# Attention and two mixture layers: thirteen block passes, token sums in the accumulator, two joined passes, eight tiles' logits on VectorE

## The chip, the cores and the metric

The kernel runs on one core of one Trainium2 chip. The metric is the device time of one execution in microseconds (us).

## The reference

x is the output of a decayed attention over blocks of 64, seen as 1536 tokens of 512. Two mixture layers follow it:

```python
out = 0                                     # first layer: 4 experts, all used
p = domain_probs / (domain_probs.sum(-1, keepdims=True) + 1e-09)
for e in range(4):                          # w1[e]: 512 x 1024, w2[e]: 1024 x 512
    out += p[:, e:e+1] * (np.maximum(x @ w1[e], 0) @ w2[e])
x = out
logits = x @ w_gate                         # second layer: 8 experts, one per token
expert_idx = argmax(logits); gate_w = softmax(logits)[expert_idx]
for e in range(8):
    out[mask_e] = gate_w * (np.maximum(x[mask_e] @ w1[e], 0) @ w2[e])
```

## The kernel before

**Numbers.** A product of two float32 operands is made of three passes of TensorE over operands split into a high and a low part (hi*hi, hi*lo, lo*hi). `hi_lo` (L170 to L172) makes the parts: ScalarE casts the high one, VectorE (in places GpSimd) subtracts it from the source. Activations stand as `xh`, `xl`, weights as `w0h`, `w0l` (first matmul) and `w1h`, `w1l` (second).

**Passes.** The first layer is 16 passes k = 0 to 15: two halves of the tokens (768 each, `TS`) by eight halves of experts (`KS`; an expert's 1024 hidden units in two halves of 512). A plain pass makes h in 4 feature blocks for a group of tokens (`moe1_mm1`, L482, printed as L469, `mm3`), splits relu(h) (`relu_split`, L476 on ScalarE and L477 on VectorE) and makes y for each tile of 128 tokens in a chain of 12 products (`moe1_mm2`, L495). VectorE adds p*y to the tile's row of `acc` (L510; the first pass of a token half writes it on ScalarE, L508). A block pass (`fast_unit`, L567) makes the same h with seven products of quarter blocks in place of eight: 14 groups of 6 matmuls of 384 columns ("b", L593), with sums of weight blocks and of token blocks as operands, and adds of the results on VectorE (L607) and ScalarE copies (L600). Its second matmul is the same. Before, `FAST` (block passes) are 2 to 7 and 9 to 13, and 0, 1, 8, 14 and 15 are plain. The weight sums of passes 10 to 13 (`KEPT`) are stored to DRAM when the first token half makes them (L225) and fetched again (L266).

**Attention** runs inside pass 0, 12 chunks of 128 tokens, each of four steps on TensorE (`att_qk` L357, `att_o` L413 and L420, `att_u` L441) set between the h and y of pass 0 by the table `paces`: the number of steps behind each of the six units of a group of 256 tokens. `att_a` multiplies the scores by the decay on VectorE (L392); `att_o` gives the chunk's tokens as two banks `xo[0]`, `xo[1]`, which become `xh`, `xl` for the first token half and are copied to `x2` (L428) for the second.

**Token sums.** The block passes need four sums of token blocks, st["t1"] to st["t4"], with their splits. `tokens_steps` makes them in the plain passes 1 and 8, with GpSimd adding xh and xl again in pass 1 (L544). `tokens_split` (L563) splits x2 into `xh`, `xl` in pass 7.

**Routing.** Logits of the token tiles of the second half: `logit_v` (L684) on VectorE multiplies an accumulator row by one of eight rows of the gate weights, held in a ring of five in the freed `x2` (`logit_load`, L679), in passes 10 to 13, for the first six tiles. The other six tiles go through `route_x` (transposes, L694) and matmuls (L707). `route_choose` (L714 to L733, seven small VectorE operations) picks the expert; `route_send` (L748 to L773) makes the rank in the expert on TensorE (`rank`), the row's place on VectorE and issues an indirect store to `bins` on GpSimd (L112). `bins` is filled once (L666) by a DMA that `open_routing` (L641) issues; the first store waits for it. In passes 14 and 15 the steps of the first six tiles go by the list `early`, one step behind each h and y; passes 14 and 15 alternate for each group of 256 tokens: h and y of 14, then of 15.

**Order.** Each engine takes its instructions in program order, so a step's place in the Python sets its place in the queue. `split_to` advances the splitting of weights, and with it the loads on SyncE (SP, L156), which also go in order. The second layer, from about 583 us, is the same in both kernels.

## Time and profile before

| | us |
|---|---|
| median of 3 runs | 757.91 (757.66 to 758.08) |
| the profiled execution | 758.02 |
| its span, first to last instruction | 756.0 |
| TensorE busy in the span | 740.2 (98%) |
| VectorE | 494.4 (65%) |
| ScalarE | 309.6 (41%) |
| GpSimd | 93.5 (12%) |

The span begins with the first instruction and ends with the last; the profiled execution is 2.0 longer. Times in rows count from the span's start. The mean granted TensorE clock is 0.997. A row of a timeline gives start, duration, engine, line and operation, output<-inputs, shapes and, in brackets, the idle time before it with what ended it. Matmuls are pipelined, so a row's duration is longer than the distance to the next; distances between starts are what one costs.

### The profile page before, as it was taken

Reading aid. Unit: us, or ns where it says so; the run is one execution under the profiler, and the core shown is the slowest. Engines: PE = TensorE matmul, PEld = TensorE weight load, DVE = VectorE, ACT = ScalarE, POOL = GpSimd, SP = SyncE. Lnnn points to the kernel's source line nnn. Section 1 sums busy time; section 2 is a strip of 40 time slices with the busy share of each in tenths; the row PEclk is TensorE's granted clock in tenths of the full one; section 3 lists DMA queues with packets and bytes.
Section 4 is the critical chain, followed back from the end, with each engine's and each line's share of the span. In section 5 each row is a group of like instructions: output and inputs, shape, how many; then the busy total and the mean of one; then the engine's idle time right before and its main releaser. Section 6 shows DMA issues by size and latency. Waiting matters only on the chain.

```text
span 756.0 us, 12472 instructions
## 1 busy us (share of the span) xinstructions
PE 740.2 (98%) x4736; PEld 667.5 (88%) x4736; DVE 494.4 (65%) x1079; ACT 309.6 (41%) x676; POOL 93.5 (12%) x98
## 2 busy tenths in 40 slices
PE   7999999999999999999999999999999999999995
PEld 7888889898898988889889898988898998998994
DVE  7444377676856767555377777777457867675883
ACT  4223335353343534345133141522124756665673
POOL 4563220000000000000000000003111013121013
PEclk9999999999999999999999999999999999999998
DMA  9774126627351122116171642286113877865660
GB/s 295 266 234 159 56 73 234 237 69 279 122 212 56 56 83 84 57 54 250 73 258 55 231 141 111 85 299 218 43 56 130 291 217 248 290 190 191 234 221 29
DMA packets 34314, 122.59 MB, mean 162 GB/s; under 512 B 4114, under 2 KB 6162, under 8 KB 31180
## 3 DMA queue, kind: packets, MB, share of 16 engines
q1 hardware_dynamic: 32139, 115.47, 44.6%
q0 software_dynamic: 2112, 6.31, 2.2%
q8 instruction: 38, 0.62, 0.3%
q14 instruction: 25, 0.20, 0.1%
HBM read 96.04 MB, written 25.92 MB: 161 GB/s over the span
## 4 chain that ended last, share of the span: by engine, by line
PE 73%; issue 17%; DVE 4%; POOL 2%; DMA 2%; ACT 1%; SPq 0%; POOLq 0%; ACTq 0%
PE y L469 35%; PE b L593 21%; PE h L469 9%; POOL out L112 2%; DMA att<-in_att 2%; PE qk L357 1%; PE xo L420 1%; PE xo L413 1%; PE z L1186 1%; DVE w1l L172 1%; PE lg L707 1%; PE u L441 0%; ACT w1h L171 0%; PE rtr L694 0%; DVE t L548 0%
## 5 line engine op out<-in xcount | busy, mean ns | idle before, releaser
L510 DVE SCALAR_TENSOR_TENSOR acc<-y,p_sb,acc 128x512 f32<-128x512 f32 x84 | 63.0, 750 | 65.3 <-PE y L469 62.1
L172 DVE TENSOR_TENSOR w1l<-raw,w1h 128x512 fp32r<-128x512 f32 x124 | 83.0, 692 | 16.6 <-ACT w1h L171 16.2
L171 ACT CAST w1h<-raw 128x512 fp32r<-128x512 f32 x128 | 75.3, 617 | 0.0
L600 ACT COPY u<-b 128x384 f32<-128x384 f32 x66 | 31.1, 475 | 100.2 <-PE b L593 98.9
L469 PE MATMUL h<-xh,w0h 128*128 128x256 f32 (+1 forms) x208 | 57.9, 308 | 1.0 <-ACT w0h L171 1.0
L172 DVE TENSOR_TENSOR w0l<-raw,w0h 128x512 fp32r<-128x512 f32 x80 | 52.5, 697 | 6.8 <-ACT w0h L171 6.3
L469 PE MATMUL h<-xh,w0l 128*128 128x256 f32 (+1 forms) x208 | 56.2, 298 | 0.0
L171 ACT CAST w0h<-raw 128x512 fp32r<-128x512 f32 x98 | 55.8, 619 | 0.3 <-DMA raw<-in_w1a 0.2
L593 PE MATMUL b<-xh,w0h 128*128 128x384 f32 x176 | 48.9, 338 | 0.0
L648 POOL IOTA places<- 128x7 f32 x1 | 0.2, 161 | 385.9 <-PE y L469 385.9
L112 POOL DMA_INDIRECT out<-y,xb x16 | 30.2, 1885 | 134.9 <-DVE y L1302 84.1
L469 PEld LDWEIGHTS h<-xh,w0h 128*128 128x128 f32 x208 | 38.2, 188 | 2.5 <-ACT w0h L171 1.2
L469 PEld LDWEIGHTS h<-xh,w0l 128*128 128x128 f32 x208 | 38.4, 189 | 0.4
L469 PE MATMUL g<-xg,w0h 128*128 128x288 f32 (+1 forms) x192 | 38.1, 293 | 0.0
L607 DVE TENSOR_TENSOR u<-b,u 128x384 f32<-128x384 f32 x66 | 36.4, 552 | 2.4 <-PE b L593 2.4
L469 PE MATMUL h<-xl,w0h 128*128 128x256 f32 (+1 forms) x208 | 37.0, 299 | 0.0
L684 DVE CUSTOM_DVE_ANT_0 x<-acc,x 128x512 f32<-128x512 f32 x48 | 32.9, 686 | 0.6
L593 PEld LDWEIGHTS b<-xh,w0h 128*128 128x128 f32 x176 | 32.3, 188 | 0.5
L469 PEld LDWEIGHTS h<-xl,w0h 128*128 128x128 f32 x208 | 31.2, 188 | 0.0
L469 PEld LDWEIGHTS g<-xg,w0h 128*128 128x128 f32 x192 | 30.8, 189 | 0.0
L593 PE MATMUL b<-xl,w0h 128*128 128x384 f32 x88 | 29.8, 339 | 0.0
L1186 PE MATMUL z<-g,w1h 128*128 128x352 f32 (+2 forms) x96 | 29.1, 366 | 0.8 <-DVE g L1208 0.7
(305 smaller groups left out, 2015.8 us busy)
## 6 DMA issues: line engine op xcount, KB each, us to landing
raw<-in_w2a SPq DMA_DIRECT2D x32, 512.0 KB, 3.6
raw<-in_w1b SPq DMA_DIRECT2D x32, 512.0 KB, 5.4
raw<-in_w2b SPq DMA_DIRECT2D x32, 512.0 KB, 4.9
att<-in_att SPq DMA_DIRECT2D x24, 512.0 KB, 5.1
raw<-in_w1a SPq DMA_DIRECT2D x22, 512.0 KB, 4.3
kept<-w0h SPq DMA_DIRECT2D x8, 1024.0 KB, 4.2
w0h<-kept SPq DMA_DIRECT2D x8, 1024.0 KB, 6.6
bins<-fill SPq DMA_DIRECT2D x1, 4626.0 KB
```

What stands on the lines that cost most here:

```text
L112: i = G.indirect_dma_start(out=dst, out_offset=bass.IndirectOffsetOnAxis(ap=idx, axis=0), in_=src, in_offset=None, bounds_check=rows - 1, ...
L171: A.copy(out=hi, in_=src)
L172: eng.tensor_tensor(out=lo, in0=src, in1=hi.bitcast(F32), op=ALU.subtract)
L357: T.matmul(qk[r][:, h, :], kT[64 * r:64 * r + 64, h, :], qT[64 * r:64 * r + 64, h, :], start=True, stop=True,)
L413: T.matmul(xo[r][o, h // 2, :], st[q, h, :], qd[q, h, :], start=h < 2, stop=False, skip_group_check=True,)
L469: T.matmul(ps, l, r, start=first and i == 0, stop=last and i == len(ops) - 1)
L510: V.scalar_tensor_tensor(out=acc[:, t, 0:DM], in0=ps, scalar=p_sb[:, t, e:e + 1], in1=acc[:, t, 0:DM], op0=ALU.mult, op1=ALU.add,)
L593: T.matmul(ps, l[:, d, c], r[:, d, :], start=first and i == 0, stop=i == len(ops) - 1, skip_group_check=not first,)
L600: A.copy(out=t, in_=bank[2, s])
L607: V.tensor_tensor(out=t, in0=bank[b, s], in1=t, op=ALU.add)
L684: V.tensor_tensor_reduce(out=x2.rearrange("p d t -> p (d t)")[:, RING * DM:], in0=acc[:, t, 0:DM], in1=logit_piece(e), scale=1.0, scalar=0 ...
L1186: T.matmul(ps[:, :2 * n], wh, both, start=i == 0, stop=False)
```

## The change

- `FAST` is 1 to 13 and `KEPT` 8 to 13. `half(k)` maps a pass to a half of an expert: the second token half goes through halves 2 to 7, 0, 1, so that passes 14 and 15 are the two halves of one expert.
- The token sums of the first half are made from a copy of xo that ScalarE puts into the unused rows 6 to 11 of `acc` (in `att_o`), by `x_sum` in pass 0; those of the second half by `x_sum` in passes 2 to 5. `sum_split` splits them in pass 0 and in pass 7, where `x_split` also splits x2.
- The last group of pass 0 sets a chunk's `att_o` right behind its `att_qk` (`paces[512]`).
- Logit rows are loaded after pass 7 and the logits of six tiles lie in passes 8 to 13.
- Passes 14 and 15 are one: per group of 256 tokens eight h, then for each tile one chain of 24 products and one update of `acc`. Routing steps go by `plan`, with hooks numbered through the 10 units of a group.
- Tiles 6 and 7 have their logits on VectorE too (`VT`), in the second group, two per hook; three more weight rows are loaded in `open_routing` ahead of the fill.

```diff
-FAST = [k for k in range(2, K1 - 2) if k != KS]
-KEPT = [k for k in FAST if k >= KS and k - KS in FAST]
+FAST = range(1, K1 - 2)
+KEPT = range(KS, K1 - 2)
+
+
+def half(k):
+    return (k + k // KS * 2) % KS
...
-VT = TT
+VT = TT + 2
...
                 hi_lo(xh[:, d, o:o + CH], xl[:, d, o:o + CH], xo[r], V)
+                A.copy(
+                    out=acc[:, TT + c, 2 * r * P:2 * r * P + 2 * P].rearrange(
+                        "p (d i) -> p d i", d=2),
+                    in_=xo[r],
+                )
...
-        wh, wl = wt[1, k]
-        parts = [((hh[:, j * P:j * P + P], hl[:, j * P:j * P + P]), (wh[:, f, :], wl[:, f, :]))
+        ws = [wt[1, k + 1 - i] for i in range(len(hs) // FC, 0, -1)]
+        parts = [((hh[:, j * P:j * P + P], hl[:, j * P:j * P + P]), tuple(w[:, f % FC, :] for w in ws[f // FC]))
...
+    def x_acc(r, j):
+        t = TT + 3 * j
+        t = acc[:, t:t + 3, 2 * r * P:2 * r * P + 2 * P]
+        return t.rearrange("p c (d i) -> p c d i", d=2)
+
+    def x_sum(n, g):
+        def x(r, j):
+            if not g:
+                return x_acc(r, j)
+            t = x2[:, 2 * r:2 * r + 2, j * TH:j * TH + TH]
+            return t.rearrange("p d (c i) -> p c d i", c=3)
+
+        a, b, op, into = {
+            3: (x(1, 1), x(0, 1), ALU.subtract, (1, 1)),
+            1: (x(0, 1), x(0, 0), ALU.subtract, (0, 1)),
+            2: (x_acc(1, 1), x(0, 0), ALU.add, (0, 0)),
+            4: (x(1, 0), x_acc(0, 0), ALU.subtract, (1, 0)),
+        }[n]
+        V.tensor_tensor(out=x_acc(*into), in0=a, in1=b, op=op)
+
+    def sum_split(n):
+        src = x_acc(*{1: (0, 1), 2: (0, 0), 3: (1, 1), 4: (1, 0)}[n])
+        hi, lo = (t.rearrange("p d (c i) -> p c d i", c=3) for t in st[f"t{n}"])
+        hi_lo(hi, lo, src, V)
+
+    def x_split(r, j):
+        d, c = slice(2 * r, 2 * r + 2), slice(j * TH, j * TH + TH)
+        hi_lo(xh[:, d, c], xl[:, d, c], x2[:, d, c], V)
...
+        rt["wg"] = rp.tile([P, E2 - RING, DM], F32, name="wg_rows", bufs=1)
+        for e in range(E2 - RING):
+            SP.dma_start(out=rt["wg"][:, e, :], in_=wgt[e:e + 1, :].to_broadcast([P, DM]))
...
+        if t >= TT and e < E2 - RING:
+            return rt["wg"][:, e, :]
...
-        paces = {0: (0, 1, 2, 2, 1, 0), 256: (1, 2, 2, 2, 1, 0), 512: (1, 2, 2, 2, 1, 0)}
...
+        paces = {0: (0, 1, 2, 2, 1, 0), 256: (1, 2, 2, 2, 1, 0), 512: (2, 2, 2, 2, 0, 0)}
...
+                elif t0 == 256:
+                    if i % 2:
+                        split_to(0, 1)
+                elif i < FC:
+                    x_sum((3, 1, 2, 4)[i], 0)
+                if t0 == 512 and i >= FC - 1:
+                    if i == FC - 1:
+                        split_to(0, 1, 2)
+                        sum_split(2)
+                    elif i == FC:
+                        split_to(0, 1, 2)
+                        sum_split(3)
+                        sum_split(1)
+                    else:
+                        split_to(0, 1, 2)
+                        sum_split(4)
...
-                elif i < 6 and k in KEPT:
+                elif k in KEPT:
+                    logit(i < 6)
+                elif i == 1 and 1 < k < 6:
+                    x_sum((3, 1, 2, 4)[k - 2], 1)
...
+                split_to(0, k + 1 + (k + 2 == KL), 2)
+                if k == KS - 1:
+                    (
+                        lambda: (x_split(0, 0), x_split(1, 0)),
+                        lambda: sum_split(2),
+                        lambda: sum_split(3),
+                        lambda: sum_split(1),
+                        lambda: (sum_split(4), x_split(1, 1)),
+                        lambda: x_split(0, 1),
+                    )[j]()
+                if k in KEPT:
                     logit(1)
-
-            def hook2(j):
-                split_to(k + 2 == KL, k + 1, 2)
-                if k == KS - 1 and j < 2:
-                    tokens_split(j)
-                if k in KEPT:
-                    logit(2)
...
+            if k == KS - 1:
+                for e in range(RING):
+                    logit_load(e)
+                logits = [(t, e) for e in range(E2) for t in range(TT)]
...
-        early = [x for t in range(TT - 2) for x in (t, None)] + [TT - 2, TT - 1]
-        for t0, n in [(t, 256) for t in range(TS, N, 256)]:
-            for k in (KL - 1, KL):
-                def units(i):
-                    if t0 + n == N and (k == KL or i >= FC - 1):
-                        split_to(0, K1)
-                    else:
-                        split_to(1, KL)
-
-                moe1_group(k, t0, n, units, early)
...
+        def route_at(t, hook):
+            at(hook, route_choose, t)
+            at(hook + 2, route_send, t)
+
+        def logits_of(t, e):
+            logit_v(t, e)
+            logit_v(t, e + 1)
+
+        for t in range(TT):
+            route_at(t, t + t // 2)
+        for t in range(TT, VT):
+            for i in range(E2 // 2):
+                at(10 + 4 * (t - TT) + i, logits_of, t, 2 * i)
+            route_at(t, 14 + 4 * (t - TT))
+        for t in range(VT, NC - 2):
+            at(20 + t - VT, route_x, t)
+            route_at(t, 21 + t - VT)
...
+            hs = []
+            for f in range(2 * FC):
+                hs.append(moe1_mm1(KL - 1 + f // FC, t0, 256, f % FC))
+                unit(f)
...
+                moe1_mm2(KL, hs, t0, j)
+                unit(2 * FC + j)
```


Three places of the order in which the engines take their instructions, before and after.

ScalarE at the start of pass 0: the four xo banks of the first two chunks and the first weight casts (xo_0 and xo_1 are a chunk's two banks, raw the loaded weights). Before:

```order
L171 CAST xh<-xo_0_247 128x2x128 [waits PE_49]
L171 CAST xh<-xo_1_248 128x2x128 [waits PE_49]
L171 CAST xh<-xo_0_269 128x2x128 [waits PE_49]
L171 CAST xh<-xo_1_270 128x2x128 [waits PE_49]
L171 CAST w0h_283<-raw_129 128x4x128 [waits DMAHW5_49]
L171 CAST w0h_283<-raw_129 128x4x128 [waits DMAHW6_49]
```

After:

```order
L177 CAST xh<-xo_0_249 128x2x128 [waits PE_49]
L438 COPY acc<-xo_0_249 128x256 [waits DVE_49]
L177 CAST xh<-xo_1_250 128x2x128 [waits PE_49]
L438 COPY acc<-xo_1_250 128x256 [waits DVE_49]
L177 CAST xh<-xo_0_273 128x2x128 [waits PE_49]
L438 COPY acc<-xo_0_273 128x256 [waits DVE_49]
L177 CAST xh<-xo_1_274 128x2x128 [waits PE_49]
L438 COPY acc<-xo_1_274 128x256 [waits DVE_49]
L177 CAST w0h_289<-raw_131 128x4x128 [waits DMAHW5_49]
L177 CAST w0h_289<-raw_131 128x4x128 [waits DMAHW6_49]
```

A copy now stands behind each cast of a bank and waits for VectorE, and all four pairs stand ahead of the casts of w0.

SP around pass 8: the loads of weights (raw), of kept sums (kept) and of logit rows (in_wgt) into x2. Before, at the end of pass 8:

```order
L156 DMA raw_3338<-in_w2a 128x1024 [waits DMAHW1_49,DVE_49,Activation_49]
L156 DMA raw_3357<-in_w2a 128x1024 [waits DMAHW2_49,DVE_49,Activation_49]
L679 DMA x_100<-in_wgt 128x512 x4
L679 DMA x_100<-in_wgt 128x512 [waits DMAHW3_49]
L156 DMA raw_3436<-in_w2a 128x1024 [waits DMAHW4_49,DVE_49]
L156 DMA raw_3477<-in_w2a 128x1024 [waits DMAHW5_49,DVE_49]
```

After, at the end of pass 7:

```order
L273 DMA w0l_1_3023<-kept_88 128x2048 [waits DMAHW3_49,DMAHW2_49,PE_49]
L273 DMA w0h_2_3043<-kept_88 128x2048 [waits DMAHW5_49]
L273 DMA w0l_3_3045<-kept_88 128x1024 [waits DMAHW6_49,DMAHW4_49,PE_49]
L689 DMA x_102<-in_wgt 128x512 [waits DVE_49]
L689 DMA x_102<-in_wgt 128x512
L689 DMA x_102<-in_wgt 128x512 [waits DMAHW7_49]
L689 DMA x_102<-in_wgt 128x512 [waits DMAHW0_49]
L689 DMA x_102<-in_wgt 128x512 [waits DMAHW1_49]
```

The five logit rows moved from behind pass 8's weights to behind the kept loads for pass 8, and the first of them now waits for VectorE.

VectorE in passes 14 and 15, first group of 256 tokens, behind the send step of a tile (pos, gs and the reciprocal end a send; mx to seen are a choose). Before:

```order
L773 RECIPROCAL acc_81<-gs0_4830 128x1 [waits DVE_49]
L714 TENSOR_REDUCE mx1_4847<-lg_v_87 128x1
L716 SCALAR_TENSOR_TENSOR sc1_4849<-lg_v_87,mx1_4847,desc_80 128x8 [waits DVE_49]
L719 TENSOR_REDUCE m2_all_83<-sc1_4849 128x1 [waits DVE_49]
L720 TENSOR_SCALAR oh1_4851<-sc1_4849,m2_all_83 128x8 [waits DVE_49]
L723 TENSOR_SCALAR ec1_4850<-m2_all_83 128x1
L727 TENSOR_SCALAR df1_4848<-lg_v_87,mx1_4847 128x8
L733 TENSOR_TENSOR seen1_4858<-seen0_4787,oh1_4851 128x8 [waits DVE_49]
L172 TENSOR_TENSOR w0l_15_4756<-raw53_4629,w0h_15_4755 128x512 [waits Activation_49]
L510 SCALAR_TENSOR_TENSOR acc_81<-y14_6_4864,p_sb_75,acc_81 128x512 [waits PE_49]
```

After:

```order
L783 RECIPROCAL acc_81<-gs1_4849 128x1 [waits DVE_49]
L724 TENSOR_REDUCE mx2_4867<-lg_v_87 128x1
L726 SCALAR_TENSOR_TENSOR sc2_4869<-lg_v_87,mx2_4867,desc_80 128x8 [waits DVE_49]
L729 TENSOR_REDUCE m2_all_83<-sc2_4869 128x1 [waits DVE_49]
L730 TENSOR_SCALAR oh2_4871<-sc2_4869,m2_all_83 128x8 [waits DVE_49]
L733 TENSOR_SCALAR ec2_4870<-m2_all_83 128x1
L737 TENSOR_SCALAR df2_4868<-lg_v_87,mx2_4867 128x8
L743 TENSOR_TENSOR seen2_4878<-seen1_4788,oh2_4871 128x8 [waits DVE_49]
L489 SCALAR_TENSOR_TENSOR ht15_768_0l_4894<-h15_768_0_4880,ht15_768_0h_4893 128x256 [waits Activation_49]
L724 TENSOR_REDUCE mx3_4897<-lg_v_87 128x1
```

Before, a choose was followed by a weight split and an accumulator update; now a choose for tile 2 stands directly behind the send for tile 1 and is followed by the remainder of an h of pass 15 and the next choose.

## Rows read from the trace of the kernel before


**Rows 1.** The page: TensorE's busy time in the span.

```profile
PE 740.2 (98%) x4736; PEld 667.5 (88%) x4736; DVE 494.4 (65%) x1079; ACT 309.6 (41%) x676; POOL 93.5 (12%) x98
```

**Rows 2.** Waits of PE: engine, line, who ended them, us, times, longest.

```profile
PE qk L357 <- DMA att<-in_att: 1.2, 2, 0.6
PE rank L748 <- DVE df L727: 0.7, 1, 0.7
```

**Rows 3.** PE timeline: first products of passes 1, 2, 8, 9, 10, 14.

```profile
81.89 0.34 PE L469 MATMUL h<-xh,w0h 128*128 128x384 f32 x1
...
116.72 0.34 PE L593 MATMUL b<-xh,w0h 128*128 128x384 f32 x1
...
305.99 0.34 PE L469 MATMUL h<-xh,w0h 128*128 128x384 f32 x1
...
341.43 0.34 PE L593 MATMUL b<-xh,w0h 128*128 128x384 f32 x1
...
372.97 0.34 PE L593 MATMUL b<-xh,w0h 128*128 128x384 f32 x1
...
499.60 0.28 PE L469 MATMUL h<-xh,w0h 128*128 128x256 f32 x1
```

**Rows 4.** PE timeline: a tile's logits and the next h, pass 14.

```profile
525.75 1.04 PE L707 MATMUL lg<-wg_sb,xt 128*128 128x8 f32 x8
...
527.03 0.36 PE L469 MATMUL h<-xh,w0h 128*128 128x256 f32 x1
```

**Rows 5.** Timelines of ACT, DVE and PE at the start of pass 0.

```profile
9.49 0.81 ACT L171 CAST xh<-xo 128x256 fp32r<-128x256 f32 x2 [7.47 <-PE xo L420]
...
11.62 1.83 ACT L171 CAST w0h<-raw 128x512 fp32r<-128x512 f32 x3
...
9.89 0.86 DVE L172 TENSOR_TENSOR xl<-xo,xh 128x256 fp32r<-128x256 f32 x2
...
12.29 0.74 PE L469 MATMUL h<-xh,w0h 128*128 128x256 f32 x4 [0.98 <-ACT w0h L171]
```

**Rows 6.** Timelines of DVE and PE in pass 0's last group.

```profile
60.51 1.29 DVE L392 TENSOR_TENSOR a<-qk,dec 128x512 f32<-128x512 f32 x2 [0.18 <-PE qk L357]
...
71.64 0.67 PE L413 MATMUL xo<-qd,st 64*64 64x128 f32 x16
```

**Rows 7.** Loads of logit rows (last three, first five); DVE, pass 10.

```profile
DMA to landing us min/median/max: 3.1/3.4/4.3
...
DMA to landing us min/median/max: 6.1/6.3/6.4
...
373.17 0.75 DVE L510 SCALAR_TENSOR_TENSOR acc<-y,p_sb,acc 128x512 f32<-128x512 f32 x1 [2.06 <-PE y L469]
...
375.93 0.69 DVE L684 CUSTOM_DVE_ANT_0 x<-acc,x 128x512 f32<-128x512 f32 x1
```

**Rows 8.** Timelines of PE (first y) and DVE, pass 14.

```profile
505.39 0.48 PE L469 MATMUL y<-w1h,ht_0h 128*128 128x512 f32 x1
...
501.70 0.42 DVE L477 SCALAR_TENSOR_TENSOR ht_0l<-h,ht_0h 128x256 fp32r<-128x256 f32 x1 [1.16 <-ACT ht_0h L476]
...
505.47 0.68 DVE L172 TENSOR_TENSOR w0l<-raw,w0h 128x512 fp32r<-128x512 f32 x1
...
506.40 0.15 DVE L755 CUSTOM_DVE_ANT_0 jk<-rank,oh 128x8 f32<-128x8 f32 x1
...
507.37 0.14 DVE L714 TENSOR_REDUCE mx<-lg_v 128x1 f32<-128x8 f32 x1
...
508.41 0.68 DVE L172 TENSOR_TENSOR w0l<-raw,w0h 128x512 fp32r<-128x512 f32 x1
```

**Rows 9.** SP's fill, GpSimd's first scatter; landing of the scatters.

```profile
496.59 0.40 SPq L666 DMA_DIRECT2D bins<-fill  x1
...
515.41 1.22 POOL L112 DMA_INDIRECT bins<-acc,pos  x1 [28.53 <-DVE ht_0l L477]
...
DMA to landing us min/median/max: 2.9/3.5/5.8
```

More of the change, by code (lines that the diff above doesn't have):

```diff
@@ L94, in body @@
     steps = const.tile([P, OMAX], F32, name="steps")
-    lg_v = const.tile([P, TT, E2], F32, name="lg_v")
+    lg_v = const.tile([P, VT, E2], F32, name="lg_v")
     sent = {"bins": [], "out": []}
@@ L142, in load_piece @@
         if k < K1:
-            src, e = (w1a, w2a)[w], k % KS // 2
+            src, e, k = (w1a, w2a)[w], half(k) // 2, half(k)
         else:
@@ L196, in body @@
     kept = {
-        k: dram.tile([len(PAIRS), P, 4, HF], F32, name=f"kept{k}") for k in FAST if k + KS in KEPT
+        k: dram.tile([len(PAIRS), P, 4, HF], F32, name=f"kept{k}") for k in map(half, KEPT)
     }
@@ L236, in third @@
         def third():
-            part("a22", raw(1, 1))
             add("s3", raw(0, 0), raw(0, 1), ALU.subtract)
@@ L243, in fourth, with plain, summed @@
             drop_raw()
-            part("s1", got["s1"])
-        return [
-            sums,
-            lambda: part("a11", raw(0, 0)),
-            lambda: part("a12", raw(1, 0)),
-            third,
-            lambda: part("s2", got["s2"]),
-            fourth,
-            lambda: part("s3", got["s3"]),
-            lambda: part("s4", got["s4"]),
+        def plain(name, d, f):
+            return lambda: part(name, raw(d, f))
+        def summed(name):
+            return lambda: part(name, got[name])
+        a11, a12, a22 = plain("a11", 0, 0), plain("a12", 1, 0), plain("a22", 1, 1)
+        s1, s2, s3, s4 = (summed(f"s{i}") for i in range(1, 5))
+        if k == 1:
+            return [a11, a12, a22, sums, s2, lambda: (third(), fourth()), s1, s3, s4]
+        return [
+            sums, a11, a12, lambda: (a22(), third()), s2, lambda: (fourth(), s1()), s3, s4,
         ]
@@ L265, in fetch @@
             m = 2 * len(names)
-            SP.dma_start(out=t[:, :m].bitcast(F32), in_=kept[k - KS][i, :, :m])
+            SP.dma_start(out=t[:, :m].bitcast(F32), in_=kept[half(k)][i, :, :m])
             for j, name in enumerate(names):
@@ L969, in att_step @@
                     at_ctx.close()
+                    open_fast()
             else:
@@ L1027, in body, with unit @@
-        for t0 in range(0, TS, 256):
-            def units(i):
-                if t0 == 0 and i < FC:
-                    split_to(1, 0, (0, 2, 1, 1)[i])
+        paces = {0: (0, 1, 2, 2, 1, 0), 256: (1, 2, 2, 2, 1, 0), 512: (2, 2, 2, 2, 0, 0)}
+        for t0 in range(0, TS, 256):
+            def unit(i):
+                for _ in range(paces[t0][i] if asteps else 0):
+                    att_step()
+                if t0 == 0:
+                    if i < FC:
+                        split_to(1, 0, (0, 2, 1, 1)[i])
@@ L1031, in units @@
                     if i == FC - 1:
                         weigh()
-                elif i % 2:
-                    split_to(1, 1)
-            moe1_group(0, t0, 256, units)
-        open_fast()
-        def plain_unit(k):
-            todo = tokens_steps(k // KS)
-            base = k // KS * TS
-            for g in range(2):
-                def units(i):
-                    if g == 0:
-                        split_to(1, k)
-                    if g == 1:
-                        split_to(0, k + 1, 2 if i == FC - 1 else 1)
-                    step = todo.pop(0) if todo else None
-                    if step:
-                        step()
-                moe1_group(k, base + g * TH, TH, units)
-            assert not any(todo)
-            split_to(0, k + 1, 8)
@@ L1056, in body @@
-        logits = []
-        for k in range(1, K1 - 2):
-            if k not in FAST:
-                plain_unit(k)
-                if k == KS:
-                    for e in range(RING):
-                        logit_load(e)
-                    logits = [(t, e) for e in range(E2) for t in range(TT)]
-                continue
+                elif t0 == 256:
[3 more added lines that the diff above has]
+                    x_sum((3, 1, 2, 4)[i], 0)
@@ L1066, in logit @@
+            for f in range(FC):
+                hs.append(moe1_mm1(0, t0, 256, f))
+                unit(f)
+            for j in range(256 // P):
+                moe1_mm2(0, hs, t0, j)
+                unit(FC + j)
+        logits = []
+        for k in FAST:
             def logit(n):
```

107 lines of the change are left out of this document (33 added, 74 removed).

## The prediction

> **What bounds the kernel now.** I read the page first: TensorE (PE) is busy 740.2 of 756.0 us [rows 1], so time goes only where PE gets less work or waits less, and any new wait on PE counts in full. Next the waits of PE: they are few and short, the two that matter here being .6 twice at qk and .7 at rank [rows 2]. Then the PE timeline at the pass boundaries [rows 3], which prices a pass. The forecast is a balance: PE work and waits that go, against waits that come, and the new waits are worked out from the other engines' queues. The sum is made against the profiled execution, 758.02 us, .1 above the median of the three runs (757.91).
>
> **What goes.**
> 1. Pass 1 becomes a block pass. A plain pass took 116.72 - 81.89 = 34.83; a block pass 372.97 - 341.43 = 31.54 [rows 3]. Saving **3.3**. (By columns, 84 products of 384 plus 72 of 512 are 69,120 columns at .456 ns, against 73,728, so only 2.1 of it is fewer columns; the rest is waiting and switching in the plain pass.)
> 2. Pass 8 becomes one: 341.43 - 305.99 = 35.44 [rows 3], saving **3.9**, again 2.1 of it columns.
> 3. Tiles 6 and 7 leave PE: transposes and logits of one tile took 527.03 - 525.75 = 1.28 (four logit products, then the next tile's four transposes) [rows 4]; two tiles **2.6**.
> 4. The .7 wait of rank [rows 2] goes with the steps it belonged to, and what takes its place is counted below: **.7**.
> Gains: 10.5.
>
> Passes 2 to 7 and 9 to 13 keep their PE work. The joined passes keep all their products; 24-step chains in place of two of 12 save six accumulator updates on VectorE (DVE), which are not on the path.
>
> **What comes.**
> A. *Token sums copied in attention.* At the start of pass 0, ScalarE (ACT) casts four xo banks in two pairs, .81 a pair, and then splits w0; the first h waits for w0h until 12.29 [rows 5]. In the new order each cast is followed by a copy of the same bank that waits for DVE's remainder (.43 each [rows 5]). Per bank: .40 cast + .43 + .40 copy = 1.2; four make 4.9, so the w0h casts begin at 9.49 + 4.9 = 14.4 instead of 11.62: 2.7 late. A late PE then finds one of qk's loads landed and gets back .6 [rows 2]: **2.1**. Bounds: .5 if copy and remainder could read the bank together (eight operations of .40 back to back from 9.49, the casts of w0 at 12.7, 1.1 late, less .6), and 2.7. The order shows the wait on DVE, so I take the high side. The Trainium skill, "PSUM — Partial Sum Buffer", section "PSUM bank collisions raise a hardware error", says that the compiler's scheduler makes any two engines that touch one bank take turns, two readers as well; by that rule the copies cost 2.1, and without it .5; no row here has a copy and a remainder on one bank. The later chunks' copies lie beside h products of 1.4 each and cost nothing on PE.
>
> B. *Pass 0, last group: xo right behind its own qk.* a is two DVE operations of 1.29 together, beginning .18 after qk [rows 6]; before, an h product of 1.4 stood between and hid them. Now only xo's qd part (.67 [rows 6]) does. The first half of a is ready .18 + .65 = .83 after qk, a wait of .2; the second comes .65 later, where PE has a little less work with the first, a wait of .1: .3 per chunk, four chunks **1.2** (bounds .8, the first wait alone, and 1.6, .1 of a semaphore more each).
>
> C. *Start of pass 1:* its first operand casts queue on ACT behind the last splits: **.1** (0 to .8, one wait like rank's).
>
> D. *Pass 8's first logit.* The weight rows go into x2, which the last split of tokens (768 wide) still reads; in the new SP order the first row's load waits for that split. DVE starts the last accumulator update .20 after the pass starts (.75, [rows 7]); the split, by the 512-wide .68 [rows 8] about 1.0, ends near 1.9; issue .3, landing 3.1 [rows 7]: the logit starts about 5.2 into the pass, where in pass 10 it started at 375.93 - 372.97 = 2.95 [rows 3, 7]. DVE and ACT are in order, so every block sum behind it is 2.2 late, and the bank that product 4 adds to is freed late; with little slack there, **2.0** reaches PE. Bounds 1.0 (slack in ACT's queue) and 4.9 (landing 6.1, as when five rows and a raw load left together [rows 7]). I take the short landing since no raw load goes just ahead. By the fit in the Trainium skill, "DMA: Bandwidth & Descriptors", section "Anatomy of one DMA — SWDGE (gpsimd) path" (2.0 us and 436 GB/s, for another issuing path), 256 KB would by estimate land in 2.6 and D be 1.5; no row here shows a landing under 2.9.
>
> E. *Joined stage, first group.* S is its first product (499.60 before [rows 3]). An h takes (505.39 - 499.60)/4 = 1.44 [rows 8]. DVE starts its first remainder at S + 2.1 (501.70 [rows 8]); then a remainder with a split takes .93, a choose step 1.04, a send step .97 [rows 8]. The y tiles, where DVE used to catch up, now come after eight h. In order: two hooks of .93 + 1.04, two of .93 + .97, then choose 2, whose one-hot is ready .8 in: 2.1 + 3.9 + 3.8 + .8 = 10.6. PE wants it after six h, at 8.6: **2.0** (bounds 1.0 and 3.0, half a step more or less). Later steps fit in the time so gained.
>
> F. *Second group.* The h part ends at S + 11.5 + 2.0 and two chains of 24 (5.6 each by columns) at S + 24.8. The fill of the bins used to be issued 3.0 before S; it now stands behind two raw loads and three weight rows that wait for the last split of pass 13's tail, near S + 4. From fill to first scatter took 515.41 - 496.59 = 18.8, and a scatter lands in 3.5 [rows 9]. Four index buffers mean that send 4 waits for scatter 0: DVE stands until S + 4 + 18.8 + 3.5 = 26.3, with send 5 and two updates behind it until 28.1, against 26.9 when the first remainder of this group could run. Then eight remainders (.33), 14 logits (.69 [rows 7]), a choose and a send: 14.3, so the last remainder is there at 42.4. PE's first chain needs it at 24.8 + 11.5 + 3.5 = 39.8: 2.6; **2.3** as the fill has fewer raw loads beside it. Bounds: 1.4 without the stall, 4.9 with the longest landing, 5.8 [rows 9].
>
> Nothing for the third group, whose routing steps are spread as before; nothing for two more stored and two more fetched halves, which use the pattern of the existing eight; nothing for the token sums in passes 2 to 5 (one DVE operation each) or for the splits in pass 7's y part (eight of about 1.0 and six updates of .75, 12.5 of the 17 us that six y tiles take by columns).
>
> **Sum.** 10.5 - (2.1 + 1.2 + .1 + 2.0 + 2.0 + 2.3) = 10.5 - 9.7 = .8. 758.02 - .8 = 757.2, as a median **757.1**. A measurement of this kernel can tell some 0.2%, 1.5 us, from no change; the forecast is inside that.
>
> **Rivals.**
> - *The joined stage holds no new wait.* DVE had the same choose, send and split steps before and PE lost .7 to them in all [rows 2]. If small steps overlap better than in my stacking, E and F fall from 4.3 to about 1: **753.8**. Against it: DVE is strictly in order and y chains no longer lie between the steps. Chance .27.
> - *Slower: the fill.* If fill and scatter 0 together end at S + 28.6 or later instead of 26.3, send 4 holds DVE for 2.3 or more on top and F reaches 4.6 to 4.9: 757.1 + 2.5 = **759.6**, over the bound; the point from which it decides is scatter 0 landing 28.6 after S. For it: 1.8 MB are queued ahead of the fill. Chance .14.
> - *The block passes do not save.* If pass 8 starts before its operands or its token splits are ready, or pass 1 waits for its own sums, the 7.2 comes back: **764.3**. Against it: pass 2 and pass 9 are such starts today, with no wait among PE's. Chance .05.
> - *Forecast:* .54, with a spread of about 2 either way from D and A: .13 of it over 0.2% faster, .36 within, .05 slower.
>
> **How the numbers follow.** Faster .27 + .13 = .40; same .36; slower .14 + .05 + .05 = .24. The range goes from the first rival to a little over the second: 753.5 to 760.2. It leaves out the third rival (.05), half of what lies beyond the second (.05) and the low end where A, B and the joined stage are all free (.08).
>
> **What would show it.** Right: pass 1 and pass 8 each near 31.6 apart from the wait; first h near 15.0 after the span's start; four waits of xo for a of .2 to .4; a wait of some 2 us of b for ACT in pass 8 with a logit of 5 us into the pass ahead of it; rank 2 waiting 2 us for DVE; first y of the second group waiting for a remainder. Wrong: copies on ACT without waits for DVE; logit rows landing before the split ends; the scatters starting before S + 20, or joined passes with PE waits under 1 us together. The forecast fails if any term is outside its bounds, above all if E and F are small, or if the waits of pass 0 grow because later chunks' copies hold up the ReLUs of h.

## The result, and the profile after

The changed kernel takes 763.72 us (median of 6 runs, 762.99 to 765.81), the kernel before 758.0 beside it (6 runs, 757.6 to 758.51): a ratio of 1.0078 [1.0065, 1.0092]. It is slower, by 5.7 us, where 757.1 was forecast and the range ended at 760.2. The profiled execution takes 763.06, its span is 761.3 (before: 756.0), its mean granted clock .994.

TensorE got less work and the kernel more time. From the page, share of the span and instructions of each engine:

```profile
PE 738.5 (97%) x4688; PEld 663.3 (87%) x4688; DVE 497.6 (65%) x1097; ACT 312.2 (41%) x684; POOL 83.2 (11%) x88
```

Against [rows 1] PE is 1.7 less busy in a span 5.3 longer. The waits of PE (line, what it waited for; total us, times, longest), to be set beside [rows 2]:

```profile
PE h L481 <- ACT w0h L177: 3.4, 1, 3.4
PE rank L758 <- DVE oh L730: 2.5, 2, 1.7
PE b L598 <- ACT u L605: 1.2, 2, 1.0
PE z L1201 <- DVE g L1223: 1.2, 2, 0.6
...
PE g L1201 <- DVE sg L1205: 0.8, 2, 0.4
PE xo L427 <- DVE a L399: 0.7, 4, 0.2
```

The first three and the last are waits that the prediction named. They are not enough to explain 5.3, so I cut the span at the starts of the stages, on the timeline of PE. The kernel before, then the changed one, first instructions of: groups 2 and 3 of pass 0 (changed: then pass 1, pass 2, pass 8, pass 9, and group 1 of the last two passes), groups 2 and 3 of the last two passes, the first and second product stage of the second layer's first expert (g and z), and its second expert:

```profile
32.79 0.28 PE L469 MATMUL h<-xh,w0h 128*128 128x256 f32 x1
57.80 0.28 PE L469 MATMUL h<-xh,w0h 128*128 128x256 f32 x1
...
524.17 0.36 PE L469 MATMUL h<-xh,w0h 128*128 128x256 f32 x1
549.93 0.37 PE L469 MATMUL h<-xh,w0h 128*128 128x256 f32 x1
583.24 0.43 PE L1186 MATMUL g<-xg,w0h 128*128 128x352 f32 x1
592.06 0.36 PE L1186 MATMUL z<-g,w1h 128*128 128x352 f32 x1
603.22 0.38 PE L469 MATMUL g<-xg,w0h 128*128 128x288 f32 x1
```

```profile
36.17 0.28 PE L481 MATMUL h<-xh,w0h 128*128 128x256 f32 x1
61.18 0.28 PE L481 MATMUL h<-xh,w0h 128*128 128x256 f32 x1
86.73 0.34 PE L598 MATMUL b<-xh,w0h 128*128 128x384 f32 x1
118.34 0.34 PE L598 MATMUL b<-xh,w0h 128*128 128x384 f32 x1
307.86 0.34 PE L598 MATMUL b<-xh,w0h 128*128 128x384 f32 x1
341.62 0.34 PE L598 MATMUL b<-xh,w0h 128*128 128x384 f32 x1
499.96 0.28 PE L481 MATMUL h<-xh,w0h 128*128 128x256 f32 x1
525.54 0.36 PE L481 MATMUL h<-xh,w0h 128*128 128x256 f32 x1
552.19 0.28 PE L481 MATMUL h<-xh,w0h 128*128 128x256 f32 x1
585.66 0.43 PE L1201 MATMUL g<-xg,w0h 128*128 128x352 f32 x1
596.39 0.40 PE L1201 MATMUL z<-g,w1h 128*128 128x352 f32 x1 [0.42 <-issue]
608.28 0.38 PE L481 MATMUL g<-xg,w0h 128*128 128x288 f32 x1
```

Differences of these starts, with [rows 3, 4] for before, against the forecast (signs: + is longer; "joined" is the stage of the last two passes):

| stretch | before | after | change | forecast |
|---|---|---|---|---|
| start to group 2 of pass 0 | 32.79 | 36.17 | +3.4 | +2.1 (A) |
| pass 0, last group | 24.09 | 25.55 | +1.5 | +1.2 (B) |
| pass 1 | 34.83 | 31.61 | -3.2 | -3.2 (1, C) |
| passes 2 to 7, together | 189.27 | 189.52 | +.25 | 0 |
| pass 8 | 35.44 | 33.76 | -1.7 | -1.9 (2, D) |
| joined, group 1 | 24.57 | 25.58 | +1.0 | +1.3 (4, E) |
| joined, group 2 | 25.76 | 26.65 | +.9 | -.3 (3, F) |
| joined, group 3, to g | 33.31 | 33.47 | +.2 | 0 |
| second layer, first expert, g | 8.82 | 10.73 | +1.9 | 0 |
| the same, z | 11.16 | 11.89 | +.7 | 0 |

The rest moves by .4 in all. Most rows came as forecast; the largest that was not foreseen at all is in the second layer, in code that the change does not touch.

### The profile page after: what moved, and what is told of

Its sections match the earlier page's. It is cut to its first block, busy times and chain, and to the rows that moved or that the text cites. A ratio compares the mean times of both kernels' runs of the same rounds, so it can differ in the third digit from the quotient of the medians.

```text
span 761.3 us, 12410 instructions
## 1 busy us (share of the span) xinstructions
PE 738.5 (97%) x4688; PEld 663.3 (87%) x4688; DVE 497.6 (65%) x1097; ACT 312.2 (41%) x684; POOL 83.2 (11%) x88
## 5 line engine op out<-in xcount | busy, mean ns | idle before, releaser
L598 PE MATMUL b<-xh,w0h 128*128 128x384 f32 x208 | 57.6, 338 | 0.0
L612 DVE TENSOR_TENSOR u<-b,u 128x384 f32<-128x384 f32 x78 | 43.1, 552 | 1.1 <-PE b L598 1.1
L694 DVE CUSTOM_DVE_ANT_0 x<-acc,x 128x512 f32<-128x512 f32 x58 | 39.7, 684 | 2.4 <-DMA x<-in_wgt 2.1
L481 PE MATMUL h<-xh,w0h 128*128 128x256 f32 x144 | 37.3, 303 | 4.0 <-ACT w0h L177 3.4
L598 PEld LDWEIGHTS b<-xh,w0h 128*128 128x128 f32 x208 | 38.2, 188 | 0.6
L481 PE MATMUL h<-xh,w0l 128*128 128x256 f32 x144 | 34.9, 285 | 0.0
L481 PEld LDWEIGHTS h<-xh,w0h 128*128 128x128 f32 x144 | 26.8, 193 | 5.9 <-ACT w0h L177 3.6
L598 PE MATMUL b<-t1h,w0h 128*128 128x384 f32 x104 | 30.9, 337 | 0.0
L598 PE MATMUL b<-t4h,w0l 128*128 128x384 f32 x104 | 29.4, 342 | 1.1 <-ACT u L605 1.0
L598 PE MATMUL b<-t3h,w0h 128*128 128x384 f32 x104 | 28.7, 337 | 0.2 <-ACT u L605 0.2
```

The source lines that it names most:

```text
L481: T.matmul(ps, l, r, start=first and i == 0, stop=last and i == len(ops) - 1)
L598: T.matmul(ps, l[:, d, c], r[:, d, :], start=first and i == 0, stop=i == len(ops) - 1, skip_group_check=not first,)
L612: V.tensor_tensor(out=t, in0=bank[b, s], in1=t, op=ALU.add)
L694: V.tensor_tensor_reduce(out=x2.rearrange("p d t -> p (d t)")[:, RING * DM:], in0=acc[:, t, 0:DM], in1=logit_piece(t, e), scale=1.0, scala ...
```

## The experiments

Each kernel is the changed one with one edit, unless said otherwise. Stage lengths are from each one's profile, that is from one execution, medians from all its runs (2 to 8); the ratio is to the kernel before run beside it (757.98 to 758.11).

| kernel | median | ratio | to group 2 | pass 8 | joined 1 | joined 2 | third, to g | g | z |
|---|---|---|---|---|---|---|---|---|---|
| the change | 763.72 | 1.0078 | 36.17 | 33.76 | 25.58 | 26.65 | 33.47 | 10.73 | 11.89 |
| a_sum_on_gpsimd | 764.68 | 1.0089 [1.0059, 1.0118] | 34.94 | 33.69 | 25.59 | 26.51 | 34.67 | 10.58 | 11.88 |
| wg_own_pool | 761.58 | 1.0051 [1.0031, 1.0071] | 36.19 | 33.94 | 25.58 | 26.81 | 33.79 | 8.82 | 11.14 |
| no_logit_in_p8_products | 761.24 | 1.0043 [1.0021, 1.0066] | 36.12 | 31.59 | 25.60 | 27.26 | 35.73 | 10.16 | 10.89 |
| index_buffers_12 | 763.1 | 1.0065 [1.0042, 1.0088] | 35.84 | 34.05 | 25.58 | 25.36 | 35.93 | 9.60 | 11.89 |
| copies_0_1_late | 760.48 | 1.0031 [1.0019, 1.0042] | 33.15 | 34.01 | 25.57 | 25.81 | 34.53 | 10.52 | 11.88 |
| warm_through_wait | 762.7 | 1.0065 [1.0042, 1.0088] | 35.08 | 33.95 | 25.57 | 26.28 | 34.51 | 10.67 | 11.87 |
| tiles_6_7_on_tensore | 760.34 | 1.0039 [1.002, 1.0059] | 36.67 | 33.91 | 25.57 | 25.70 | 33.42 | 8.82 | 11.16 |
| old_pace_alone | 763.17 | 1.0068 [1.005, 1.0087] | 36.46 | 34.04 | 25.59 | 25.97 | 33.65 | 10.62 | 11.88 |
| four_parts_mended | 751.76 | .9915 [.9903, .9927] | 32.90 | 31.54 | 23.48 | 25.86 | 36.57 | 9.89 | 10.80 |
| xe_load_earlier | 751.43 | .9913 [.9899, .9926] | 32.71 | 31.54 | 23.48 | 25.86 | 33.36 | 8.82 | 11.17 |
| warm_before_rows | 753.26 | .9937 [.9919, .9956] | 32.72 | 31.54 | 23.48 | 25.86 | 35.04 | 8.82 | 11.62 |
| xe_earlier_old_pace | 751.57 | .9915 [.9901, .9928] | 32.49 | 31.54 | 23.48 | 25.86 | 33.36 | 8.82 | 11.15 |

A stage length of one execution has a scatter of its own. In the six kernels whose start is that of the changed one the first h begins at 14.5 to 15.4, and group 2 of pass 0 at 35.8 to 36.7. In the seven whose joined stage is that of the changed one (the change, a_sum_on_gpsimd, wg_own_pool, no_logit_in_p8_products, copies_0_1_late, warm_through_wait, old_pace_alone), group 2 takes 25.8 to 27.3 and the third, to g, 33.5 to 35.7. So a difference that lies within these spans shows nothing by itself.

### The second layer: wg_own_pool

In the changed kernel ScalarE's first copy of g's result stands still, not for TensorE but for the last indirect stores. ACT timeline of the changed kernel, then of this one:

```profile
589.98 0.31 ACT L1204 COPY sg<-g 128x176 f32<-128x176 f32 x1 [4.12 <-DMA bins<-acc,pos]
```

```profile
587.76 0.30 ACT L1204 COPY sg<-g 128x176 f32<-128x176 f32 x1 [1.21 <-PE g L1202]
```

The edit moves the three weight rows out of the routing pool's front into memory of their own:

```diff
-        rt["wg"] = rp.tile([P, E2 - RING, DM], F32, name="wg_rows", bufs=1)
+        rt["wg"] = rt_ctx.enter_context(pool("wgp", 1, side="right")).tile([P, E2 - RING, DM], F32, name="wg_rows")
```

> The changed kernel, but the three extra weight rows lie in a pool of their own opened behind the routing pool, so that the tiles of the routing pool keep their old places. Theory (the rows moved a tile that a scatter reads to where the second layer's first buffer lies, so ScalarE's first copy there waits for the last scatter to land): the first expert's g stage of the second layer takes 8.8 instead of 10.73 and z 11.2 instead of 11.89; the time falls by 2.6 us to about 761.1. Rival (the first expert's weights are split late because the last group of the joined passes leaves VectorE behind): g and z stay as they are, time within 0.5 us of 763.7.

g takes 8.82 and z 11.14 again, as before (8.82, 11.16), and the median falls by 2.1; the wait is TensorE's 1.21, and everything else of the table stays within .35. So the added rows pushed the routing pool's small tiles along, and sg came to lie where the last stores still read: a wait by memory, not by data. That the last stores read just there is inferred from the copy's wait; that the rows' place makes the wait is shown, by this run and by tiles_6_7_on_tensore, which has no such rows.

### The start: warm_through_wait, copies_0_1_late, a_sum_on_gpsimd

ScalarE's timeline at the start of pass 0 in the changed kernel shows term A as it was stacked: each copy waits for VectorE to have read the bank.

```profile
9.63 0.37 ACT L177 CAST xh<-xo 128x256 fp32r<-128x256 f32 x1 [7.62 <-PE xo L427]
10.50 0.37 ACT L438 COPY acc<-xo 128x256 f32<-128x256 f32 x1 [0.49 <-DVE xl L178]
10.77 0.38 ACT L177 CAST xh<-xo 128x256 fp32r<-128x256 f32 x1
11.64 0.37 ACT L438 COPY acc<-xo 128x256 f32<-128x256 f32 x1 [0.49 <-DVE xl L178]
...
14.18 2.18 ACT L177 CAST w0h<-raw 128x512 fp32r<-128x512 f32 x4
```

That is the taking of turns on one bank that the Trainium skill states for the compiler's scheduler ("PSUM — Partial Sum Buffer", section "PSUM bank collisions raise a hardware error"); the trace agrees: each copy waits .49 for VectorE. But PE, having stood still 3.35, then works at a lower clock (PE timeline: the first h, and the step behind the second h):

```profile
14.86 0.96 PE L481 MATMUL h<-xh,w0h 128*128 128x256 f32 x4 [3.35 <-ACT w0h L177]
...
19.41 0.69 PE L453 MATMUL u<-att,kd 128*64 128x64 f32 x16
```

Two h take 19.41 - 14.86 = 4.55; before, 3.07 (12.29 to 15.36). `warm_through_wait` keeps PE at work in the wait, with 50 products that nothing reads:

```diff
+        warmup(ps_mm.tile([P, 512], F32, tag="mm", name="warm2"), 50)
```

> The changed kernel with fifty small products that nothing reads, on TensorE behind the xo of chunk 1, so that it is busy through the wait for w0h. Theory (part of the loss at the start is the granted clock, 0.91 in the first 20 us, which falls because TensorE stands still for 3.35 us): the first h still begins near 14.9, but the granted clock stays at 1.00, the first two h take 3.1 instead of 4.55 and the second group begins near 34.7 instead of 36.17; time falls by 1.5 us to about 762.2. Rival (the first h are slow because their weights or VectorE come late): no change in the first two h.

The row of 15 to 20 us (busy time of PE, PEld, DVE, ACT, POOL, then the granted clock, DMA share, GB/s) in the changed kernel, and in this one:

```profile
15.00:20.00 5.00, 5.00 (x40) 4.83 (x40) 1.86 (x4) 2.23 (x6) 2.97 (x2) 0.66 0.65 249
```

```profile
15.00:20.00 5.00, 4.76 (x49) 4.56 (x50) 2.77 (x6) 3.54 (x8) 3.83 (x3) 1.00 0.72 271
```

The clock stays at 2.4 GHz, where the changed kernel's falls to 1.2 for part of the stretch, and the two h take 3.07 again (15.24 to 18.31). From the first h to group 2 it takes 19.84 in place of 21.31, the whole 1.5; since the first h begins .4 later, which is within the scatter of such starts, group 2 is reached 1.1 earlier. The median is 1.0 lower.

`copies_0_1_late` takes away the copies of the first two chunks alone; GpSimd makes their sums again from xh and xl behind the second group's y.

```diff
-                A.copy(
+                if c >= B: A.copy(
...
+                    if i in (4, 5):
+                        x_back(i - 4)
```

> The changed kernel, but the token sums' copies of chunks 0 and 1 alone are taken off ScalarE's start: GpSimd makes them as xh + xl in the y part of pass 0's second group; chunks 2 to 5 stay on ScalarE. Theory (only the copies ahead of the w0 casts cost, by 2.6 of delay and by the clock that falls in the long idle time; the run with all six chunks on GpSimd lost its gain to GpSimd's queue): first h near 12.5, second group of pass 0 begins near 33.0 instead of 36.17, third 58.0, and the time falls by 3.2 us to about 760.5. Rival (copies of chunks 2 to 5, or any copy on GpSimd, cost as much): second and third group begin within 1 us of 36.2 and 61.2.

```profile
12.80 0.74 PE L493 MATMUL h<-xh,w0h 128*128 128x256 f32 x4 [0.98 <-ACT w0h L177]
```

The wait is 1.0 as before the change, group 2 is reached at 33.15 (3.0 earlier), and the median falls by 3.2: both the delay and the clock belong to these four copies, and the other chunks' copies cost PE nothing. `a_sum_on_gpsimd` moves all copies there, at once:

```diff
-                A.copy(
+                G.tensor_tensor(
...
-                    in_=xo[r],
+                    in0=xh[:, d, o:o + CH].bitcast(F32), in1=xl[:, d, o:o + CH].bitcast(F32), op=ALU.add,
```

> The changed kernel, but the copy of xo into the accumulator is made by GpSimd as xh + xl in place of ScalarE's copy. Theory (the copies' turns with VectorE on each bank hold up the casts of w0, and the long idle time lets the clock fall): ScalarE is through its four casts by 11.6, the first h begins near 12.3 instead of 14.86, the granted clock of the first 20 us is 1.00 instead of 0.91, the second group of pass 0 begins near 32.9 instead of 36.17, and the time falls by 3.2 to 3.4 us to about 760.3. Rival (the first h waits for landing weights or for another engine): first h stays at 14 or later and the time within 1 us of 763.7.

The first h starts at 12.62, but three new waits appear in PE's list, and the time is 764.68 (2 runs), no better than the change:

```profile
PE xo L420 <- POOL qd L375: 1.3, 2, 0.7
...
PE y L481 <- DVE w1l L178: 1.1, 1, 1.1
...
PE h L481 <- POOL w0l L178: 0.8, 1, 0.8
```

GpSimd's queue also makes qd and parts of the weights in pass 0, and there the copies are in the way of those. Where the work is put matters less than what is queued behind it.

### The pace of pass 0: old_pace_alone

```diff
-... 512: (2, 2, 2, 2, 0, 0)}
+... 512: (1, 2, 2, 2, 1, 0)}
-                    if i == FC - 1:
+                    if i == FC:
```

(with the splits moved behind the y products in the same way).

> The changed kernel with only the old pace in the last group of pass 0 and the splits for pass 1 in its y part. Theory: third group 24.1 instead of 25.55, pass 1 31.6 to 32.0, time falls by 1.1 to 1.4 to about 762.4. Rival: third group and pass 1 together 57 or more, time as changed, 763.7.

The last group takes 24.09 again, so B is the pace's. But pass 1 then takes 33.4 in place of 31.6, with a wait of 1.55 for a copy on ScalarE that stands behind the casts of t1 to t4, done between 84.8 and 90.0. Both together: 57.5, against 57.2 with the new pace. The pace pays for itself and gives nothing.

### Pass 8: no_logit_in_p8_products

In the changed kernel the first logit starts 312.96 - 307.86 = 5.1 into the pass (5.2 forecast), and PE pays at product 4 (DVE, then PE):

```profile
312.96 0.69 DVE L694 CUSTOM_DVE_ANT_0 x<-acc,x 128x512 f32<-128x512 f32 x1 [2.06 <-DMA x<-in_wgt]
```

```profile
321.49 0.44 PE L598 MATMUL b<-t4h,w0l 128*128 128x384 f32 x1 [1.01 <-ACT u L605]
```

```diff
-                    logit(i < 6)
+                    logit(k > KS and i < 6)
```

> The changed kernel without the three logits among the products of pass 8; they go to later passes. Theory (the first logit waits for the landing of its row, and the block sums behind it on VectorE hold up product 4): pass 8 takes 31.6 to 31.7 instead of 33.76 and the time falls by 2.1 us to about 761.6. Rival (pass 8 waits for its fetched weight sums or its late token splits): pass 8 keeps 33 or more.

Pass 8 takes 31.59 as any block pass: D is 33.76 - 31.59 = 2.2 (2.0 forecast). The wait at product 4 is 1.0 of it, where the prediction looked for some 2; against pass 9, PE falls behind at three places, .5 at 315.63, .4 at 319.18 and 1.2 here, each behind a copy u on ScalarE. The median falls by 2.5. In the profile, the longest of the three runs (762.21; the others 761.24 and 761.12), groups 2 and 3 of the joined stage are .6 and 2.3 longer; the last of the experiments look at the third.

### The joined stage: index_buffers_12, tiles_6_7_on_tensore

PE's waits for rank, in groups 1 and 2, VectorE's stand for the first store, which ends with the landing of what GpSimd issued at 524.32, and VectorE's last remainder of group 2:

```profile
510.95 0.17 PE L758 MATMUL rank<-oh,upper 128*128 128x8 bf16 x1 [1.69 <-DVE oh L730]
...
538.10 0.17 PE L758 MATMUL rank<-oh,upper 128*128 128x8 bf16 x1 [0.78 <-DVE oh L730]
```

```profile
527.59 0.15 DVE L781 CAST pos<-pf 128x1 int32<-128x1 f32 x1 [6.40 <-DMA bins<-acc,pos]
...
543.88 0.42 DVE L489 SCALAR_TENSOR_TENSOR ht_3l<-h,ht_3h 128x256 fp32r<-128x256 f32 x1
```

PE's other long waits in group 2, from the same list as above (ht_2l and ht_3l are remainders):

```profile
PE h L481 <- DVE ht_2l L489: 0.6, 1, 0.6
PE y L481 <- DVE ht_3l L489: 0.5, 1, 0.5
```

The fill, for which the first store waits, on SP's timeline:

```profile
503.94 0.43 SPq L674 DMA_DIRECT2D bins<-fill  x1
```

With twelve index buffers in place of four no send waits for an earlier store:

```diff
-        pos = rt["rp"].tile([P, 1], I32, tag="pos", name=f"pos{t}", bufs=4)
+        pos = rt["rp"].tile([P, 1], I32, tag="pos", name=f"pos{t}", bufs=12)
```

> The changed kernel with twelve index buffers in place of four, so that no send waits for an earlier scatter to land. Theory (the stall of VectorE behind the fill sets the waits of the second group): the second group of the joined passes falls from 26.65 to about 25.0, the time by 1.3 to 1.7 us to about 762.2. Rival (sixteen logits in the h part bind VectorE anyway): the group stays above 26.2 and the time within 0.5 us of 763.7.

Group 2 takes 25.36, 1.3 less than in the changed kernel's profile: the stand's price there. In the seven kernels that have the stand it ends 27.3 to 28.8 after the stage's start; against their group 2 of 25.8 to 27.3 the price is .5 to 1.9. But group 3 with the tail takes 2.5 more, and the median is only .6 lower (763.1, 3 runs). The waits and a row of the windows of this kernel say how:

```profile
PE px L804 <- DMA xe<-bins: 1.1, 1, 1.1
```

```profile
580.00:585.00 5.00, 4.53 (x38) 4.54 (x38) 3.12 (x23) 0.30 (x2) 0.00 (x0) 0.70 0.03 9
```

PE waits for the load of the first expert's rows (xe) from bins, and then works at a clock of .70. It is not the issue of this load that lags. The changed kernel's, then this one's:

```profile
575.18 0.37 SPq L791 DMA_DIRECT2D xe<-bins  x1
```

```profile
573.82 0.37 SPq L791 DMA_DIRECT2D xe<-bins  x1
```

Both are issued 23.0 after the start of group 3, so the load is 1.4 earlier, as PE is. In the changed kernel PE uses the rows 5.3 after the issue without a wait; here they are there only after 6.7. The same load, issued at the same place, makes PE wait .1 or less in the change, old_pace_alone and tiles_6_7_on_tensore, .2 in wg_own_pool, .6 in no_logit_in_p8_products, and .9 to 1.1 in warm_through_wait, copies_0_1_late and a_sum_on_gpsimd. Why it takes longer to land in some executions is not shown, and so it is not shown either that the loss follows from the gain ahead of it.

`tiles_6_7_on_tensore` gives the two tiles back to PE, in group 2, and drops the three rows:

```diff
-VT = TT + 2
+VT = TT
...
-            at(20 + t - VT, route_x, t)
-            route_at(t, 21 + t - VT)
+            hook = 10 * (t // 2 - 2) + t % 2
+            at(hook, route_x, t)
+            route_at(t, hook + 1)
```

> The changed kernel with tiles 6 and 7 back on the transposes and logit products of TensorE, hooks 10 to 13, and without the three extra weight rows. Theory (sixteen logits and the stall on VectorE cost the second group more than the 2.6 that TensorE is spared; the extra rows are what moved the buffer on which the second layer waits): the second group of the joined passes is 25.5 to 26.0 instead of 26.65, the first expert's g and z of the second layer 8.8 and 11.2 instead of 10.73 and 11.89; time falls by about 3.4 us to 760.3. Rival (the logits on VectorE are a gain that only the index buffers spoil): second group above 27.

The median falls by 3.4. g and z are those of before, and group 2 takes 25.70 although PE has 2.6 more to do in it: the two tiles on VectorE had cost 26.65 - (25.70 - 2.6) = 3.5 in this group (2.7 to 4.2 by the seven kernels' group 2), more than they took from PE.

### All mended, and the tail: four_parts_mended, xe_load_earlier, warm_before_rows, xe_earlier_old_pace

`four_parts_mended` joins copies_0_1_late, no_logit_in_p8_products and tiles_6_7_on_tensore, and sets the stores behind the choosing of the next tiles:

```diff
-            at(hook + 2, route_send, t)
+            at(hook + 4, route_send, t)
```

(with more buffers for df, ec, oh and pos, the last in memory of their own).

> The changed kernel with: chunks 0 and 1 copied late by GpSimd; no logits among pass 8's products; tiles 6 and 7 back on TensorE; sends four hooks behind their choose, with six index buffers outside the routing pool. Theory (the account by stages adds up): first h near 12.5, pass 8 31.6, first joined group 23.5 to 24.0 instead of 25.58, second 25.5 to 26, second layer's first expert 8.8 and 11.2; together 3.2 + 2.1 + 1.8 + .9 + 2.6 = 10.6 less, about 753.1, below the kernel before. Rival (a gain ahead of the tail is lost there, as in two runs: the load of the first expert's rows is not earlier, TensorE waits for it and the clock falls): two or more us of it come back between the last group and the second layer, about 755.5.

The median is 751.76 (8 runs, 751.14 to 755.34), 1.3 less than expected. Group 1 takes 23.48: E was 25.58 - 23.48 = 2.1 (2.0 forecast), no wait for rank is left. Third group and tail take 36.57 in its profile, where the changed kernel has 33.47; the waits, the loads on SP and the windows of this kernel:

```profile
PE px L813 <- DMA xe<-bins: 1.4, 1, 1.4
```

```profile
555.05 10.89 SPq L162 DMA_DIRECT2D raw<-in_w2b  x3
566.25 0.38 SPq L800 DMA_DIRECT2D xe<-bins  x1
```

```profile
575.00:580.00 5.00, 4.91 (x35) 4.65 (x32) 3.04 (x20) 1.21 (x5) 1.95 (x2) 0.55 0.14 53
```

The load is issued 22.8 after the group's start, as it was, and lands 7.0 later. SP is in order, and the rows' load stands behind weight loads. `xe_load_earlier` adds to it one move, the load ahead of the y of tile 10:

```diff
-                    first_load()
...
+                if last:
+                    first_load()
                 moe1_mm2(KL, hs, t0, j)
```

> The run with four parts mended, and the load of the first expert's rows (xe) is issued one y tile earlier, ahead of a weight load on SP. Theory (TensorE waits 1.4 for that load ahead of the second layer, and the clock then falls to half for some 7 us): the stretch from the last group's start to the second layer is 33.3 to 33.7 instead of 36.57, g and z of the first expert 8.8 and 11.2 instead of 9.89 and 10.80, granted clock 1.00 there; time falls by 3.5 us to about 748.3. Rival (the rows wait for the scatters, not for SP's order): the wait for xe stays above 1 and the time at 751.8.

```profile
564.50 0.38 SPq L800 DMA_DIRECT2D xe<-bins  x1
```

```profile
575.00:580.00 5.00, 4.86 (x41) 4.78 (x40) 4.37 (x22) 2.90 (x10) 1.95 (x2) 1.00 0.28 107
```

The wait is gone from the list, the load is 1.6 earlier in the group, the clock is 1.00, and the tail takes 33.36 (-3.2). Yet the median is only .3 lower, 751.43, within each other's intervals. So the profiled execution of four_parts_mended, with its long tail, was not like its median one: it is the longest of the 8 (755.34), the others lie between 751.14 and 751.92. The 5 runs with the earlier load lie between 751.22 and 751.63; that the move prevents such a long execution is likely, but five runs don't show it, since seven of eight had none without it. `warm_before_rows` left the load and added products ahead of the wait:

```diff
-        keep_up(8)
+        keep_up(40)
```

> The run with four parts mended, with forty small products in place of eight on TensorE ahead of the first expert's rows. Theory (of the loss ahead of the second layer only 1.4 is the wait itself, the rest the clock that falls after it): the rows are transposed no earlier, but the clock stays at 1.00 from 570 to 585, the stretch to the second layer is 34.3 to 34.8 instead of 36.57, and the first expert's g is 8.8; time falls by 2.5 us to about 749.3. Rival (the stretch is long for another reason, such as VectorE's steps of the last two tiles): stretch above 36, time unchanged or longer by the added products.

The clock holds here too and g takes 8.82, but the tail takes 35.04 and the median is 753.26 (2 runs): the added products cost more than they saved. Last, `xe_earlier_old_pace` sets the old pace of pass 0 into xe_load_earlier:

> The run with the load of xe earlier, and the last group of pass 0 at the old pace (xo one h behind its qk), with the sums for pass 1 split in its y part. Theory (TensorE waits .3 a chunk for VectorE's product of scores and decay, and pass 1's splits fit in the y part): the third group of pass 0 is 24.1 instead of 25.55, pass 1 31.6 to 32.0, time about 747.2. Rival (the splits no longer fit, and pass 1 or its start pays): third group and pass 1 together 57 or more as now, time about 748.3.

751.57 against 751.43: the pace is a trade here as well. `xe_load_earlier` is the best of these, faster than both kernels: 6.7 below before, 12.3 below the change.

## Why the prediction was wrong

**What held.** Gains 1 and 2 (3.2 measured in pass 1, and 31.54 to 31.59 for pass 8 without its logits, 3.9 less than before); term C (nothing to be seen); D in place, cause and size, 2.2 for 2.0, with the landing at 3.1 us as taken from [rows 7] rather than the 2.6 that the prediction worked out from the Trainium skill's fit; E, 2.1 for 2.0; the delay of the first h in A, 14.86 - 12.29 = 2.6 for 2.7; B, 1.5 for 1.2, inside its bounds, with the four waits at xo that it named (.18 each).

**The step that failed most: the second layer was not in the sum.** The text prices nothing behind the third group, and what stands ahead of it calls the second layer the same in both kernels. Its instructions are; their waits are not. Three rows at the front of a pool moved the tiles behind them, and 2.6 us came in at sg and z. That is nearly half of the 5.3.

**A was mis-sized**: 3.4 for 2.1 (3.0 to 3.9 in the six kernels with this start), beyond its bound of 2.7. It counted the time PE would stand (right), and took none for the lower clock after it: 4.55 - 3.07 = 1.5 for two h. The .6 it took back at qk did come back.

**F was mis-sized**: 3.5 for 2.3, within its bounds. The stand on VectorE was there (6.40, and 1.3 in PE's time by index_buffers_12); it ended 527.59 - 499.96 = 27.6 after the stage's start, 26.3 by the text. The fill was issued 4.0 after the start, as forecast; what the text had too short is the way from it to the first store, 524.32 - 503.94 = 20.4 for 18.8. (Its step from 26.3 to 28.1 is too short as well by its own prices: a send of .97 and two updates of .75 make 2.5, not 1.8.) The last remainder was there at 44.3 in place of 42.4. F was worked out from this one alone; in fact PE lost time in several places of the group: .6 at h, .78 at rank and .5 at y stand among the rows above, and the whole came out only from the stage's length. So gain 3, right as TensorE's work, was a loss in total.

**Small ones:** .25 in passes 2 to 7 and .2 in pass 8. From the forecast of -.8: second layer 2.6, A 1.3, F 1.2, B .3, these two .4, group 1 of the joined stage less .3 (E itself was as forecast, but the group without its waits is .4 shorter than before), the rest .6, makes 5.3.

**The rivals.** *No new wait* fell with PE's list of waits. *The fill* did not decide as put: the stand ended at 27.6, short of 28.6 (27.3 to 28.8 in the seven kernels that have it, over 28.6 in one); its side was the right one, mostly for other reasons. *Block passes do not save* is refuted; its 764.3 came nearest to the measured time by a wrong mechanism.

## What to carry to other kernels

A tile added at the front of a pool moves all that follow; look at which waits of untouched code change, above all where a later stage takes over memory that an indirect store still reads. A wait of TensorE can cost half as much again by the clock behind it (3.35 of wait, 1.5 more over the next two h). And a load that is issued just in time makes a stage as long as its landing happens to take: here the same load, issued at the same place, cost TensorE nothing in one profile and 1.4 and a low clock in another. Compare several executions before a difference in such a stage is put down to an edit.
